# One of three GpSimd additions of a weight-product pair moved to VectorE, with the activation and the low half as steps of their own and attention units placed one by one

## The chip, the cores and the metric

One core of one Trainium2 chip runs the whole program in one launch. The metric is the device time in microseconds, the median of the runs. PE is TensorE, DVE is VectorE, ACT is ScalarE, POOL is GpSimd, and SP is the engine whose queue issues all the transfers.

## What is computed

Two stages in float32: an attention over q, k, v (8 batches, 8 heads, 576 positions, 64 wide), then a gated feed-forward layer.

```python
q_d, k_d, v_d = means over 4 neighbouring positions
out_d = softmax(q_d @ k_d.T / 8) @ v_d, repeated 4 times along the positions
out_local = softmax(masked(q @ k.T / 8, |i - j| < 4)) @ v
x = (out_up + out_local) as 4608 tokens x 512
y = (sigmoid(x @ w_gate) * (x @ w_val)) @ w_out        # 512 -> 1536 -> 512
```

## The kernel before, in words

**Units and batches.** The attention is done in 32 units of two heads (four units to a batch of 576 tokens). A unit's steps are named: `prep2`, `s0`, `s1`, `sm` (scores of the local part and their softmax), `d0`, `d1`, `dn` (the coarse part), `vd`, `v` (preparing v; `v` splits it into a high and a low float16 half, L191 on ACT and L192 on DVE, tile `vblk`), `a0`, `a1`, `at`, `od`, `x` (the two products, and the split of the result into float16 halves, L600 to L628). A float32 product of the feed-forward layer is three float16 matmuls (high by high, high by low, low by high).

**Batches 0 and 1** multiply the gate and value weights plainly (`moe_gate`, `moe_val`), while the weights are loaded, scaled and split (batch 0) and summed for what follows (batch 1, `sums`, L736 to L746).

**Batches 2 to 7** use a scheme with seven products in place of eight for a 2 by 2 block. `pair(b, n)` does one such block: n runs from 0 to 11, even n for the gate (PSUM tiles `pg`), odd n for the value (`pv`), two chunks of 128 hidden columns each. The seven products P1, P6, P7, P2, P5, P3, P4 are seven groups of six matmuls; in the rows a group is named by two digits: 00, 44, 55, 11, 33, 62, 26 in that order (`pg_4_5_44` is product P6 of batch 4's sixth gate pair). Each group's result is a 128 by 288 PSUM tile. ACT copies the first three to SBUF (L789, L792, L796, tiles of `arena` named `sx`), and DVE adds the other four from PSUM (L782, `plus`). Three additions have both operands in SBUF and run on POOL (also L782): P6's copy plus P1's, P7's copy plus that sum, and the fourth result from the second. At the end of an even pair ACT takes a tanh; at the end of an odd pair DVE multiplies (L679), ACT writes the high half of the product (L191) and DVE the low half (L192) into `gq`, which the output product reads.

**PSUM.** All groups of the layer take turns in five PSUM buffers (`ps_m`), the attention's other products in three (`ps_a`), so a group must wait until the group five before it has been read.

**Order.** After a batch's 12 pairs come its output products `po` (288 matmuls, tiles m = 0 to 3, halves h = 0, 1; L700 to L709). The four units of batch b+1 run meanwhile, between the groups of batch b. Every step stands at a position from the table `T` (`add(pos, f)`): a batch starts at `start(b)`, a pair's steps are a seventh of a pair apart, and a unit's step stands at the batch's start plus a number of its unit (`c0` to `c3`) plus a number of the step that all units share (`ms0`, `ms1`, ...). The steps are issued in that order, and a scheduler then fixes the order on each engine. Each engine works its own queue in order.

The lines that the argument uses: L413 (all products), L478, L489, L496 to L500 (local softmax), L521 to L541 (coarse softmax), L187 (largest value of v), L782 (`plus`), L192, L679.

## Time and profile before

| | us |
|---|---|
| median of 3 runs | 1086.05 |
| range of the runs | 1085.66 to 1088.92 |
| the profiled execution | 1082.34 |
| its span, first to last instruction | 1080.4 |
| PE busy in the span | 1025.9 (95%) |
| DVE busy | 744.7 (69%) |
| POOL busy | 610.7 (57%) |
| ACT busy | 488.1 (45%) |

[...] The profiled execution is 3.71 us shorter than the median. Matmuls are pipelined and their ends are modelled, so that PE can look busy through a short wait. In the views below, PEld is the loading of weights into PE. A busy share over the whole span mixes stages with different limits, so the windows by stage say more than the totals.

### The profile page before, as it was taken

The numbers are of one execution on the slowest core, as the hardware profiler recorded it, in microseconds if no ns is written. First come the engines' busy times: TensorE is split into PE (matmuls) and PEld (weight loads), VectorE is DVE, ScalarE is ACT, GpSimd is POOL, SyncE is SP. The second block draws the span as 40 slices with busy tenths as digits, with TensorE's granted clock in tenths as the row PEclk, the third lists the DMA queues.
The fourth block names the chain that finished last, engine by engine and source line by source line (L and its number), as shares of the span: only waits on it lengthen the run. The fifth ranks groups of instructions, "written<-read, shape, count | busy, mean of one in ns | idle before, by whom it ended". The sixth has DMA issues, their size and how long they took to land.

```text
span 1080.4 us, 23529 instructions
## 1 busy us (share of the span) xinstructions
PE 1025.9 (95%) x9511; PEld 810.3 (75%) x9511; DVE 744.7 (69%) x1366; ACT 488.1 (45%) x1089; POOL 610.7 (57%) x647
## 2 busy tenths in 40 slices
...
GB/s 371 138 234 269 279 140 122 110 120 125 122 109 186 171 206 190 81 134 223 182 166 121 142 211 182 120 129 170 211 175 112 131 217 152 107 34 114 171 46 34
DMA packets 64188, 168.99 MB, mean 156 GB/s; under 512 B 25040, under 2 KB 31312, under 8 KB 64080
## 3 DMA queue, kind: packets, MB, share of 16 engines
...
## 4 chain that ended last, share of the span: by engine, by line
PE 58%; DVE 19%; POOL 9%; issue 5%; ACT 5%; DMA 3%; SPq 0%; POOLq 0%; DVEq 0%; ACTq 0%
PE po L413 26%; PE pg L413 11%; PE pv L413 10%; POOL arena L782 4%; PE x L413 3%; PE s L413 2%; PE od L413 2%; POOL t L490 2%; DVE vm L187 1%; PE sd L413 1%; DVE arena L782 1%; DMA qkd<-in_qkd_dram 1%; DVE arena L742 1%; DVE tanh L679 1%; DVE gq L192 1%
## 5 line engine op out<-in xcount | busy, mean ns | idle before, releaser
L413 PEld LDWEIGHTS <-arena 128*128 128x128 f16 x4176 | 404.7, 98 | 129.5 <-issue 13.9
L413 PE MATMUL pg<-arena 128*128 128x288 f16 x2088 | 282.4, 290 | 12.2 <-DVE arena L782 5.2
L413 PE MATMUL po<-gq,wo 128*128 128x288 f16 x2304 | 292.1, 287 | 0.4 <-DVE arena L782 0.3
L413 PE MATMUL pv<-arena 128*128 128x288 f16 x2088 | 281.8, 287 | 2.0 <-DVE arena L782 0.6
L413 PEld LDWEIGHTS <-wo 128*128 128x128 f16 x2304 | 224.9, 98 | 58.1 <-issue 1.0
L782 POOL TENSOR_TENSOR arena<-arena 128x288 f32<-128x288 f32 x198 | 195.5, 995 | 67.8 <-ACT arena L792 52.4
L782 DVE TENSOR_TENSOR arena<-pv,arena 128x288 f32<-128x288 f32 x144 | 62.6, 444 | 59.1 <-POOL arena L782 49.2
L705 DVE TENSOR_SCALAR arena<-po,osc 128x288 f32<-128x288 f32 x32 | 16.5, 515 | 102.7 <-PE po L413 102.7
L192 DVE SCALAR_TENSOR_TENSOR vblk<-v,svb,vblk 64x640 f16<-64x640 f32 x48 | 76.0, 1583 | 4.2 <-ACT vblk L191 3.4
L490 POOL TENSOR_TENSOR t<-t,mx 128x640 f32<-128x640 f32 x32 | 49.6, 1551 | 51.5 <-DVE mx L489 51.0
L402 POOL TENSOR_TENSOR qkd<-qkd 128x576 f32<-128x576 f32 x29 | 39.0, 1345 | 51.3 <-DMA qkd<-in_qkd_dram 51.1
L191 ACT ACTIVATE gq<-tanh 128x576 f16<-128x576 f32 (+1 forms) x42 | 37.4, 890 | 62.6 <-DVE tanh L679 62.6
L288 POOL TENSOR_TENSOR arena<-arena 128x512 f16<-128x512 f32 x24 | 37.0, 1562 | 44.2 <-ACT arena L287 44.1
L413 PEld LDWEIGHTS s<-qk 64*64 64x64 f32 x1200 | 43.4, 137 | 17.6 <-issue 15.1
L192 DVE SCALAR_TENSOR_TENSOR gq<-tanh,gq 128x576 f16<-128x576 f32 (+1 forms) x42 | 52.8, 1256 | 4.0 <-ACT gq L191 4.0
L413 PE MATMUL s<-qk 64*64 64x64 f32 x1200 | 54.4, 227 | 0.0
L500 POOL TENSOR_TENSOR t<-t,sm 128x640 f32<-128x640 f32 x27 | 36.1, 1340 | 31.6 <-DVE sm L498 26.0
L413 PE MATMUL sd<-kdblk,qks 128*72 128x288 f32 x128 | 43.2, 420 | 10.3 <-DVE t L478 6.1
L707 ACT ACTIVATE arena<-po,osc 128x288 f32<-128x288 f32 x32 | 16.0, 500 | 81.6 <-PE po L413 62.4
L541 POOL TENSOR_TENSOR ad<-e,sme 72x288 f32<-72x288 f32 x50 | 33.4, 688 | 27.7 <-DVE sme L532 19.2
L524 ACT ACTIVATE e<-sd,mxd 72x144 f32<-72x144 f32 x128 | 46.9, 369 | 1.4
L191 ACT ACTIVATE vblk<-v,svb 64x640 f16<-64x640 f32 x48 | 39.6, 825 | 12.3 <-DVE svb L184 6.0
...
## 6 DMA issues: line engine op xcount, KB each, us to landing
...
```

Of the source, the lines that this page charges most:

```text
L191: nc.scalar.activation(hi, src, AF.Copy, scale=sc)
L192: return nc.vector.scalar_tensor_tensor(out=lo, in0=src, scalar=sc, in1=hi, op0=ALU.mult, op1=ALU.subtract)
L288: nc.gpsimd.tensor_tensor(out=lo, in0=a, in1=hi, op=ALU.subtract)
L402: nc.gpsimd.tensor_tensor(out=x[:, :, 0:2], in0=x[:, :, 0:2], in1=x[:, :, 2:4], op=ALU.add)
L413: nc.tensor.matmul(o, w[a], x[c], start=first and i == 0, stop=last and i == len(pairs) - 1)
L490: nc.gpsimd.tensor_tensor(out=t, in0=t, in1=mx.unsqueeze(2).to_broadcast([P, NBLK, WIN]), op=ALU.subtract)
L500: eng.tensor_tensor(out=t, in0=t, in1=sm.unsqueeze(2).to_broadcast([P, NBLK, WIN]), op=ALU.mult)
L524: nc.scalar.activation(s["e"][:, qb, h, :], pt[:QM, h * SD : (h + 1) * SD], AF.Exp, bias=mx[:, h : h + 1], scale=QKSCALE / 16, accum_out=s ...
L541: eng.tensor_tensor(out=AD[:, qb].rearrange("p c h k -> p h c k")[:, :, :, :KC], in0=s["e"][:, qb].rearrange("p h (c k) -> p h c k", c=NKC ...
L705: nc.vector.tensor_scalar(out=dst_, in0=pt[:, :HN], scalar1=sc, scalar2=None, op0=ALU.mult)
L707: nc.scalar.activation(dst_, pt[:, :HN], AF.Copy, scale=sc)
L782: eng.tensor_tensor(out=dst_, in0=x, in1=y, op=ALU.add)
```

## The change

In `pair`, the sum of P6 and P1 is one DVE addition that reads P6 from PSUM; the ACT copy and the POOL addition that did it are gone. P5's sum goes to `sx[:, 0]` and no longer into the result tile. The tanh, or the multiplication and the high half, become an eighth step (`act`) and the low half a ninth (`low`), placed 0.3 and 1.8 sevenths of a pair behind step `s4`'s place (rounded), so behind the first groups of the next pair. The output product starts with three pieces of ten chunks (m, h = 0,0; 0,1; 1,0) and then does the last two chunks of each; before, it started with two. In the table, the four units of a batch have their own 14 numbers each.

Other numbers that moved: the last output weight's place `j35` and the start of batch 1 `T1` are both 2.37 earlier, the places of two units with them; the first unit's steps are 0.83 later; eight matmuls on an idle tile stand at position 44 (`an3=8`). The engine of a few single operations of batches 0 and 1 changes: unit 1's coarse normalisation goes from ACT to DVE (`ae1`), unit 4's from DVE to ACT (`ae4`), units 2's and 6's from ACT to POOL; the local normalisation of units 3 and 6 goes from POOL to DVE (`te3`, `te6`).

```diff
         def s6():
-            nc.scalar.copy(sx[:, 1], go(P6))
-            plus(sx[:, 1], sx[:, 1], sx[:, 0], nc.gpsimd)
+            plus(sx[:, 1], go(P6), sx[:, 0])
...
         def s5():
-            plus(j["c"][:, 1], go(P5), sx[:, 1])
-            plus(j["c"][:, 3], j["c"][:, 1], sx[:, 2], nc.gpsimd)
+            plus(sx[:, 0], go(P5), sx[:, 1])
+            plus(j["c"][:, 3], sx[:, 0], sx[:, 2], nc.gpsimd)
 
         def s3():
-            plus(j["c"][:, 1], go(P3), j["c"][:, 1])
+            plus(j["c"][:, 1], go(P3), sx[:, 0])
 
         def s4():
             plus(j["c"][:, 2], go(P4), sx[:, 3])
+
+        def act():
             t = tg[b, p]
...
             act_val(t, j["c"])
-            del tg[b, p]
-            split(*[gq[:, 2 * p : 2 * p + 2, e].rearrange("p f (h c) -> p f h c", h=2) for e in range(2)],
-                  t.rearrange("p (f h) c -> p f h c", f=2), GSC)
-
-        return s1, s6, s7, s2, s5, s3, s4
+            nc.scalar.activation(gpart(p, 0), halves(t), AF.Copy, scale=GSC)
+
+        def low():
+            if k:
...
+                nc.vector.scalar_tensor_tensor(
+                    out=gpart(p, 1), in0=halves(tg.pop((b, p))), scalar=GSC, in1=gpart(p, 0), op0=ALU.mult, op1=ALU.subtract)
+
+        return s1, s6, s7, s2, s5, s3, s4, act, low
...
-        return start(b) + T[f"c{hp}"] * span(b - 1) / 126 + T["m" + k]
+        return start(b) + T[f"m{hp}{k}"] * span(b - 1) / 118
...
-                add(t0 + GP * i / 7, f)
+                add(t0 + GP * (i / 7 if i < 7 else (6.01 + (T["da"] if i == 7 else T["da"] + T["dl"])) / 7), f)
...
-        add(t0, lambda b=b, f=part: f(b, 0, 0, range(10)))
-        add(t0 + 0.4 * u0, lambda b=b, f=part: f(b, 0, 1, range(10)))
-        add(t0 + 0.8 * u0, lambda b=b, f=part: f(b, 0, 0, range(10, 12)))
-        add(t0 + 0.9 * u0, lambda b=b, f=part: f(b, 0, 1, range(10, 12)))
...
+        for i in range(3):
+            add(t0 + 0.4 * u0 * i, lambda b=b, i=i, f=part: f(b, i // 2, i % 2, range(10)))
+        for i in range(3):
+            add(t0 + (1.2 + 0.1 * i) * u0, lambda b=b, i=i, f=part: f(b, i // 2, i % 2, range(10, 12)))
```

**Place 1: DVE in the value pair 4 of batch 4** (`pv_4_4`; units 20 to 23 are the next batch's, and the pairs of batches 3, 5 and 6 read alike). Before:

```order
L600 TENSOR_TENSOR arena_109<-x_21_0_8556,od16_21_8512 128x464
L600 TENSOR_TENSOR arena_109<-x_21_8_8582,od16_21_8512 128x112
L192 SCALAR_TENSOR_TENSOR vblk_129<-v22_7472,svb_139,vblk_129 64x10x64
L782 TENSOR_TENSOR arena_109<-pv_4_4_33_8597,arena_109 128x288
L478 SCALAR_TENSOR_TENSOR t_23_8619<-s_23_0_8606,mk_108 128x384
L192 SCALAR_TENSOR_TENSOR vblk_129<-v22_7472,svb_139,vblk_129 64x10x64
L187 TENSOR_REDUCE vm6_9206<-v24_9068 128x1
L478 SCALAR_TENSOR_TENSOR t_23_8619<-s_23_3_8621,mk_108 128x256
L605 TENSOR_TENSOR arena_109<-arena_109 128x2x288
L187 TENSOR_REDUCE vm6_9206<-v25_9107 128x1
L489 TENSOR_REDUCE mx_23_8631<-t_23_8619 128x10
L782 TENSOR_TENSOR arena_109<-pv_4_4_26_8643,arena_109 128x288
```

After the change, the same pair from its first addition to the same last one:

```order
L783 TENSOR_TENSOR arena_109<-pv_4_4_44_8492,arena_109 128x288
L783 TENSOR_TENSOR arena_109<-pv_4_4_11_8509,arena_109 128x288
L783 TENSOR_TENSOR arena_109<-pv_4_4_33_8517,arena_109 128x288
L783 TENSOR_TENSOR arena_109<-pv_4_4_62_8530,arena_109 128x288
L478 SCALAR_TENSOR_TENSOR t_23_8551<-s_23_0_8538,mk_108 128x384
L478 SCALAR_TENSOR_TENSOR t_23_8551<-s_23_3_8553,mk_108 128x256
L489 TENSOR_REDUCE mx_23_8563<-t_23_8551 128x10
L783 TENSOR_TENSOR arena_109<-pv_4_4_26_8567,arena_109 128x288
```

What stood there of unit 21's result (`x_21`, L600, L605), of unit 22's split (`vblk`) and of the next v (L187) has gone to other places. Unit 21's result and unit 22's split now stand in the last pair, `pv_4_5`:

```order
L600 TENSOR_TENSOR arena_109<-x_21_0_8678,od16_21_8590 128x464
L600 TENSOR_TENSOR arena_109<-x_21_8_8704,od16_21_8590 128x112
L783 TENSOR_TENSOR arena_109<-pv_4_5_44_8719,arena_109 128x288
L192 SCALAR_TENSOR_TENSOR vblk_129<-v22_7449,svb_139,vblk_129 64x10x64
L783 TENSOR_TENSOR arena_109<-pv_4_5_11_8736,arena_109 128x288
L192 SCALAR_TENSOR_TENSOR vblk_129<-v22_7449,svb_139,vblk_129 64x10x64
L521 TENSOR_REDUCE mxd_23_1_8859<-sd_23_1_8857 72x2
L605 TENSOR_TENSOR arena_109<-arena_109 128x2x288
L550 TENSOR_TENSOR at16_22_8671<-at_22_3_8821,at16_22_8671 128x232
L783 TENSOR_TENSOR arena_109<-pv_4_5_33_8749,arena_109 128x288
L605 TENSOR_TENSOR arena_109<-arena_109 128x4x288
L783 TENSOR_TENSOR arena_109<-pv_4_5_26_8766,arena_109 128x288
```

Behind these, the output product of the batch begins on PE.

**Place 2: DVE in the value pair 2 of batch 4** (`pv_4_2`), where unit 20's result comes and unit 21's v is split. Before:

```order
L600 TENSOR_TENSOR xs_113<-x_20_0_8150,od16_20_8113 128x464
L600 TENSOR_TENSOR xs_113<-x_20_8_8176,od16_20_8113 128x112
L192 SCALAR_TENSOR_TENSOR vblk_129<-v21_7470,svb_139,vblk_129 64x10x64
L782 TENSOR_TENSOR arena_109<-pv_4_2_11_8196,arena_109 128x288
L192 SCALAR_TENSOR_TENSOR vblk_129<-v21_7470,svb_139,vblk_129 64x10x64
L605 TENSOR_TENSOR arena_109<-xs_113,arena_109 128x288
L782 TENSOR_TENSOR arena_109<-pv_4_2_33_8204,arena_109 128x288
```

After the change:

```order
L600 TENSOR_TENSOR xs_113<-x_20_0_8118,od16_20_8116 128x464
L783 TENSOR_TENSOR arena_109<-pv_4_2_44_8104,arena_109 128x288
L600 TENSOR_TENSOR xs_113<-x_20_8_8144,od16_20_8116 128x112
L192 SCALAR_TENSOR_TENSOR vblk_129<-v21_7447,svb_139,vblk_129 64x10x64
L521 TENSOR_REDUCE mxd_21_1_8224<-sd_21_1_8222 72x2
L192 SCALAR_TENSOR_TENSOR vblk_129<-v21_7447,svb_139,vblk_129 64x10x64
L605 TENSOR_TENSOR arena_109<-xs_113,arena_109 128x288
L783 TENSOR_TENSOR arena_109<-pv_4_2_11_8164,arena_109 128x288
L531 TENSOR_SCALAR sme_21_8067<-sme_21_8067 72x4
L783 TENSOR_TENSOR arena_109<-pv_4_2_33_8172,arena_109 128x288
```

The addition of group 44 (L783) is new, and a reduction of unit 21's coarse scores (L521) has come in between the two halves of the split.

**Place 3: DVE in batch 1**, ahead of the scores of unit 11 (`s_11_0`), around the value product of hidden chunk 6. Before:

```order
L605 TENSOR_TENSOR arena_109<-arena_109 128x2x288
L679 SCALAR_TENSOR_TENSOR tanh_112<-tanh_112,pv_1_6_1_3590 128x288
L605 TENSOR_TENSOR arena_109<-arena_109 128x4x288
L187 TENSOR_REDUCE vm3_4293<-v12_4155 128x1
L192 SCALAR_TENSOR_TENSOR gq_111<-tanh_112,gq_111 128x576
L742 TENSOR_TENSOR arena_109<-arena_109 128x256 x2
L187 TENSOR_REDUCE vm3_4293<-v13_4163 128x1
L187 TENSOR_REDUCE vm3_4293<-v14_4243 128x1
L478 SCALAR_TENSOR_TENSOR t_11_3648<-s_11_0_3635,mk_108 128x384
```

After the change:

```order
L679 SCALAR_TENSOR_TENSOR tanh_112<-tanh_112,pv_1_6_1_3544 128x288
L743 TENSOR_TENSOR arena_109<-arena_109 128x256
L187 TENSOR_REDUCE vm3_4257<-v12_4156 128x1
L192 SCALAR_TENSOR_TENSOR gq_111<-tanh_112,gq_111 128x576
L187 TENSOR_REDUCE vm3_4257<-v13_4158 128x1
L747 TENSOR_TENSOR arena_109<-arena_109 128x4x256
L478 SCALAR_TENSOR_TENSOR t_11_3606<-s_11_0_3593,mk_108 128x384
```

Unit 9's result (L605 twice) and one reduction of v (L187) no longer stand ahead of unit 11's scores.

## Rows read from the trace of the kernel before

**Rows 1.** The page's first part, the whole span: busy time and share of each engine, and its instructions.

```profile
PE 1025.9 (95%) x9511; PEld 810.3 (75%) x9511; DVE 744.7 (69%) x1366; ACT 488.1 (45%) x1089; POOL 610.7 (57%) x647
```

**Rows 2.** Windows by stage: start and end of the stretch, its length, then busy time and instructions of PE, PEld, DVE, ACT, POOL, then granted clock, DMA share, GB/s. The stages are batch 0, batch 1 with its output, the pairs and output of batches 2, 3, 4, 5, 6, the pairs of batch 7, and its output.

```profile
0.00:206.00 206.00, 182.40 (x1599) 144.68 (x1600) 172.28 (x377) 118.15 (x278) 113.03 (x116) 0.94 0.63 215
206.00:356.50 150.50, 143.14 (x1369) 114.08 (x1369) 115.89 (x194) 60.76 (x130) 74.25 (x67) 0.98 0.36 123
356.50:481.00 124.50, 121.04 (x1163) 95.53 (x1162) 85.15 (x153) 56.73 (x132) 84.42 (x89) 1.00 0.48 166
481.00:605.80 124.80, 120.98 (x1162) 95.09 (x1161) 83.84 (x149) 56.32 (x126) 78.26 (x88) 1.00 0.47 161
605.80:730.60 124.80, 120.95 (x1162) 95.09 (x1160) 85.67 (x149) 56.32 (x126) 78.07 (x88) 1.00 0.47 162
730.60:855.95 125.35, 121.15 (x1161) 95.14 (x1160) 83.78 (x149) 56.32 (x126) 77.90 (x88) 1.00 0.47 160
855.95:979.60 123.65, 119.11 (x1118) 93.51 (x1117) 77.44 (x136) 54.16 (x120) 70.10 (x76) 1.00 0.36 124
979.60:1041.40 61.80, 61.80 (x505) 49.25 (x504) 34.79 (x57) 26.22 (x47) 33.29 (x35) 1.00 0.40 139
1041.40:1080.40 39.00, 35.34 (x289) 27.98 (x286) 5.87 (x9) 3.16 (x5) 1.40 (x2) 1.00 0.09 31
```

**Rows 3.** Windows of batch 4, the same columns: first and last quarter of its pairs, and all its pairs.

```profile
605.80:626.50 20.70, 20.70 (x192) 15.82 (x190) 15.55 (x32) 9.55 (x21) 14.37 (x19) 1.00 0.58 192
667.80:690.00 22.20, 18.46 (x191) 14.29 (x189) 21.70 (x31) 12.38 (x32) 15.71 (x18) 1.00 0.42 151
605.80:690.00 84.20, 80.35 (x754) 61.93 (x752) 67.95 (x117) 45.41 (x106) 64.90 (x72) 1.00 0.54 186
```

**Rows 4.** Timeline of PE at the end of the pairs of batch 4: start, duration, instruction; in brackets the idle time before it and what ended it.

```profile
674.99 0.90 PE L413 MATMUL pg<-arena 128*128 128x288 f16 x6 [0.97 <-DVE arena L782]
...
677.90 0.71 PE L413 MATMUL sd<-kdblk,qks 128*72 128x288 f32 x2 [1.20 <-DVE t L478]
...
680.83 1.63 PE L413 MATMUL pg<-arena 128*128 128x288 f16 x12 [0.76 <-DVE arena L782]
```

**Rows 5.** Timeline of DVE in the same stretch; the split of v (`vblk`) is the second row.

```profile
668.68 0.81 DVE L600 TENSOR_TENSOR arena<-x,od 128x464 f32<-128x464 f32 x2
669.67 4.90 DVE L192 SCALAR_TENSOR_TENSOR vblk<-v,svb,vblk 64x640 f16<-64x640 f32 x1 [0.17 <-ACT vblk L191]
...
674.86 0.54 DVE L478 SCALAR_TENSOR_TENSOR t<-s,mk 128x384 f32<-128x384 f32 x1
675.43 1.23 DVE L192 SCALAR_TENSOR_TENSOR vblk<-v,svb,vblk 64x640 f16<-64x640 f32 x1
...
677.43 0.41 DVE L478 SCALAR_TENSOR_TENSOR t<-s,mk 128x256 f32<-128x256 f32 x1
...
679.61 0.80 DVE L489 TENSOR_REDUCE mx<-t 128x10 f32<-128x640 f32 x1
680.34 0.44 DVE L782 TENSOR_TENSOR arena<-pv,arena 128x288 f32<-128x288 f32 x1
```

**Rows 6.** Timeline of POOL in the same stretch.

```profile
669.73 0.79 POOL L782 TENSOR_TENSOR arena<-arena 128x288 f32<-128x288 f32 x1
...
673.83 1.39 POOL L628 TENSOR_TENSOR arena<-arena 128x288 f32<-128x288 f32 x1
```

**Rows 7.** Timeline of DVE earlier in the same batch: the second half of another unit's split, and the low half of a result.

```profile
644.08 0.89 DVE L192 SCALAR_TENSOR_TENSOR vblk<-v,svb,vblk 64x640 f16<-64x640 f32 x1
645.00 0.94 DVE L605 TENSOR_TENSOR arena<-xs,arena 128x288 f16<-128x288 f32 x1
```

**Rows 8.** Groups by line of DVE in the pairs of batch 4: count, busy time, mean ns of one, idle time before and what ended it.

```profile
L782 DVE TENSOR_TENSOR arena<-pv,arena 128x288 f32<-128x288 f32 x20 | 8.8, 442 | 4.3 <-POOL arena L782 4.3
```

**Rows 9.** Groups by line of POOL (first) and of ACT (second) in the same stretch.

```profile
L782 POOL TENSOR_TENSOR arena<-arena 128x288 f32<-128x288 f32 x32 | 31.2, 984 | 7.7 <-ACT arena L792 4.4 <-DVE arena L782 2.2 <-ACT arena L796 0.4
...
L792 ACT COPY arena<-pv 128x288 f32<-128x288 f32 x6 | 2.4, 402 | 0.3 <-PE pv L413 0.3
```

**Rows 10.** Waits in the pairs of batch 4: total, times, longest.

```profile
DVE arena L782 <- POOL arena L782: 4.6, 7, 1.4
```

**Rows 11.** The chain that ended last, in the pairs of batch 7: start, duration, instructions.

```profile
1000.17 5.14 PE pg L413 x42
```

**Rows 12.** Windows of batch 1, columns as in the second group.

```profile
297.00:310.00 13.00, 8.63 (x58) 6.22 (x57) 12.22 (x23) 5.26 (x13) 4.44 (x5) 0.87 0.11 42
258.00:271.00 13.00, 10.34 (x101) 7.60 (x99) 10.24 (x14) 3.93 (x7) 7.57 (x9) 0.87 0.47 149
```

**Rows 13.** Waits of PE in batch 1: total, times, longest.

```profile
PE at L556 <- DVE t L478: 4.4, 1, 4.4
```

**Rows 14.** Windows of batch 0, columns as in the second group.

```profile
52.00:156.00 104.00, 91.46 (x751) 69.68 (x749) 100.36 (x223) 55.40 (x112) 54.19 (x42) 0.95 0.73 230
156.00:169.00 13.00, 9.82 (x90) 8.64 (x89) 11.96 (x24) 8.87 (x23) 7.89 (x10) 0.73 0.31 107
```

**Rows 15.** Groups by line of DVE over the span: the local and the coarse normalisation that run on DVE now.

```profile
L500 DVE TENSOR_TENSOR t<-t,sm 128x640 f32<-128x640 f32 x5 | 4.9, 972 | 0.1
...
L541 DVE TENSOR_TENSOR ad<-e,sme 72x288 f32<-72x288 f32 x2 | 1.9, 974 | 0.0
```

More of the change, by code (lines that the diff above doesn't have):

```diff
@@ L692, in out_group @@
     def out_group(b, m, h, pt, fcs):
+        assert issued(b, "v", fcs)
         for fc in fcs:
@@ L785, in s1 @@
             ready()
+            assert all((b, i, "act") in seen for i in range(n - 1)) and all((b, "v", 2 * i) in seen for i in range(p - 1))
             if k == 0:
@@ L802, in s5 @@
         def s5():
-            plus(j["c"][:, 1], go(P5), sx[:, 1])
-            plus(j["c"][:, 3], j["c"][:, 1], sx[:, 2], nc.gpsimd)
+            plus(sx[:, 0], go(P5), sx[:, 1])
+            plus(j["c"][:, 3], sx[:, 0], sx[:, 2], nc.gpsimd)
         def s3():
-            plus(j["c"][:, 1], go(P3), j["c"][:, 1])
+            plus(j["c"][:, 1], go(P3), sx[:, 0])
         def s4():
             plus(j["c"][:, 2], go(P4), sx[:, 3])
+        def act():
             t = tg[b, p]
+            seen.add((b, n, "act"))
             if k == 0:
@@ L815, in s4, with halves, gpart @@
             act_val(t, j["c"])
-            del tg[b, p]
-            split(*[gq[:, 2 * p : 2 * p + 2, e].rearrange("p f (h c) -> p f h c", h=2) for e in range(2)],
-                  t.rearrange("p (f h) c -> p f h c", f=2), GSC)
-        return s1, s6, s7, s2, s5, s3, s4
+            nc.scalar.activation(gpart(p, 0), halves(t), AF.Copy, scale=GSC)
+        def low():
+            if k:
+                seen.update((b, "v", 2 * p + i) for i in range(2))
+                nc.vector.scalar_tensor_tensor(
+                    out=gpart(p, 1), in0=halves(tg.pop((b, p))), scalar=GSC, in1=gpart(p, 0), op0=ALU.mult, op1=ALU.subtract)
+        return s1, s6, s7, s2, s5, s3, s4, act, low
+    def halves(t):
+        return t.rearrange("p (f h) c -> p f h c", f=2)
+    def gpart(p, e):
+        return gq[:, 2 * p : 2 * p + 2, e].rearrange("p f (h c) -> p f h c", h=2)
     steps = {}
@@ L854, in attention_moe @@
             add(T[f"aw{i}"], lambda n=T[f"an{i}"]: awake(n))
-    for g in ("p0", "p1", "p2", "p3", "q", "m"):
+    for g in ("p0", "p1", "p2", "p3", "q", "m0", "m1", "m2", "m3"):
         for chain in ("s0 s1 sm a0 a1 x", "prep2 d0 d1 dn at od x", "vd od", "v x"):
@@ L867, in attention_moe @@
             continue
-        p0 = at(u, "s0") - T["qs0" if b == 1 else "ms0"]
+        p0 = at(u, "s0")
         add(max(at(u - 2, "s1") + 0.1, p0 - T["lk"]), lambda u=u: load_qk(u))
@@ L871, in attention_moe @@
         add(max(at(u - 1, "vd") + 0.1, p0 - T["ll"]), lambda u=u: load_vd(u))
-        pb = start(b) + T["c0"] * span(b - 1) / 126
+        pb = start(b) + T["m0s0"] * span(b - 1) / 118
         pl = max(at(u - 4, "v") + 0.1, T["v4"] + T["vs4"] * hp if b == 1 else pb + T["vv"] + T["vvs"] * hp)
```

7 lines of the change are left out of this document (3 added, 4 removed).

## Prediction

> **What bounds the kernel now.** The page's totals say PE: 95% busy against 69% for DVE and 57% for POOL [rows 1]. That is an average, so I went on to the windows by stage. The pairs of batch 7 and its output have no attention beside them, and there PE is busy for 61.80 of 61.80 us; nothing is to be gained there. In the five stretches before, PE is idle for 3.46, 3.82, 3.85, 4.20 and 4.54 us (length less PE busy): 19.87 us together. Batch 1 has 150.5 - 143.14 = 7.36 us of idle PE, batch 0 has 206 - 182.40 = 23.6 [rows 2].
>
> Where in a batch is this idle time? The windows of batch 4 answer: its first quarter of pairs has none, its last has 22.20 - 18.46 = 3.74 of the 3.85, and in that quarter DVE is busy for 21.70 of 22.20 us, 98% [rows 3]. PE's timeline there shows gaps of 0.97, 1.20 and 0.76 us, each ended by a DVE instruction [rows 4]. So PE is the bound in most of a batch, and DVE in a short stretch. DVE's timeline shows why: from 668.68 to 680.78 it works off unit 21's result, both halves of unit 22's split, unit 23's scores and three reductions between the additions that free PSUM [rows 5]. One half of the split takes 4.90 us, while POOL runs without a pause from 669.73 to 675.22 [rows 6]; another takes 0.89 [rows 7]. What I read from these: a DVE split can be held while POOL adds, and the five PSUM buffers do not cover 12 us of late additions.
>
> **The change, part by part.**
>
> *One POOL addition and one ACT copy less, one DVE addition more, 72 times.* A POOL addition takes 984 ns and P6's copy 402 ns [rows 9]; a DVE addition from PSUM takes 442 ns [rows 8]. In a batch of 12 pairs POOL loses 11.8 us, ACT 4.8, and DVE gains 5.3. None of it is PE time. ACT's 4.8 us give nothing by themselves: ACT is busy for 45.41 of 84.20 us of pairs [rows 3]. POOL's part shortens a chain: DVE waited 4.6 us in 7 waits for POOL's additions in a batch's pairs [rows 10], and the first of the two sums that P5 and P7 need is now DVE's own. DVE's 5.3 us fit if spread: its load goes from 67.95 to 73.3 of 84.20 us [rows 3].
>
> *The units placed one by one.* This is the part that I expect to pay. In the stretch of place 1 DVE has now only five additions, two score steps and a maximum: 5 x 0.44 + 0.54 + 0.41 + 0.80 = 3.95 us [rows 5], against a pair's 42 matmuls in 5.14 us [rows 11], so DVE keeps up and the three gaps go. What stood there stands in the last pair, whose twelve shown rows need about 0.50 + 0.81 + 4 x 0.44 + 2 x 0.89 + 0.44 + 1.20 + 1.34 + 0.40 = 8.2 us (rows 5 and 7 where they have the operation; L605's two at most 2.5, the small ones estimated as an addition each), or 12.2 with one split stretched by 4.90 - 0.89 = 4.0. Behind it PE has the rest of that pair, 36 matmuls, and then 60 matmuls of output before a group needs the buffer of group 33: 96 x 0.1224 = 11.8 us [rows 11]; the addition of 33 stands about 6 us into that list, 10 if stretched. This cover is why the heap costs nothing there. If the output's pieces were short of buffers, it would cost the excess, at most 1 us a batch.
>
> *A new narrow place.* In place 2 the addition of group 11 stands behind unit 20's result, the new addition of 44, a reduction, both halves of a split and a low half: 0.81 + 0.44 + 0.89 + 0.44 + 0.89 + 0.94 + 0.44 = 4.85 us [rows 5, 7]. PE asks for that buffer when it has done 55, 11, 33, 62, 26 and the next pair's 00: 36 matmuls, 4.4 us [rows 11], and some 0.6 us of attention products: 5.0. The slack is about 0.2 us. If no split is held, the new wait is 0; if one is held by 4.0, it is 3.8. Before, the second half of this place's split took 0.89 [rows 7], but POOL starts on the result at the same moment. I take the middle, 1.9 a batch, and keep both ends. Sum of batches 2 to 6: -19.9 + 5 x 1.9 = **-10.4** (ends -19.9 and -0.9).
>
> *Low half as a step of its own.* DVE now has an addition to do while ACT writes the high half; this is inside DVE's idle time and costed at nothing. Three pieces of output ahead of the last two chunks give the last low half 90 matmuls of cover, not 60 (11.0 against 7.3 us [rows 11]); the number of matmuls is the same.
>
> *Batch 1.* [...] I count the gap and its clock as gone: **-6.1**. The second gap, in 258 to 271, is 2.66 us and 1.7 of clock [rows 12]; it may go too (end: -10.5) or neither may (end: 0). The three additions a pair do not occur in this batch.
>
> *Batch 0.* Here DVE is busy for 100.36 of 104 us from 52 to 156 [rows 14], so what counts is DVE work. Unit 4's coarse normalisation leaves it: 2 x 0.974 = 1.9 us; unit 6's local one comes, 0.97 [rows 15]; units 1 and 3 lie before 52. Net **-1.0**. The eight idle matmuls stand ahead of a product that waits for weights; uncovered they cost at most 8 x 0.12 = 1.0. The other end is set by the clock: in 156 to 169 it was 0.73, 3.5 us lost [rows 14]. A moved gap can take that away or add it again: -4.5 to +3.5.
>
> *Queues.* POOL's unit steps are moved among its additions, and it waits for the next `qkd` from memory as before; the load is issued about 1.2 of the table's units earlier relative to the unit, and the one of `vd` about 8 earlier, both behind the previous unit's use of the same buffer. On SP the loads of the next v, two of which wait for DVE's splits, now stand between the weight loads singly. I cost these at 0; the cover is the three buffers of weights.
>
> **Sum:** -10.4 - 6.1 - 1.0 = -17.5 against the profiled execution's 1082.34: 1064.8. The runs' median is 3.71 above that execution; carried over, the forecast is 1086.05 - 17.5 = **1068.5 us**.
>
> **Rivals.**
>
> *The narrow place of each batch is hit in full* (0.20). For it: DVE has 5.3 us more, and the half of a split that met POOL took 4.90. Against it: POOL has 11.8 us less. Then batches 2 to 6 give 0.9 only, and the time is 1086.05 - 0.9 - 6.1 - 1.0 = **1078**.
>
> *DVE becomes the bound of the pairs, and the time grows* (0.12). DVE's pairs now are 67.95 busy and 16.25 idle [rows 3]. With 5.3 more, the stretch stays at 84.2 only if 5.3 of that idle time goes; that is the point from which it decides. If only the 4.6 us of waits for POOL go [rows 10], a batch grows by 0.7, five by 3.5: **1090**; if none goes, by 26, 1112. For it: the 98% of the last quarter. Against it: in the other three quarters DVE is at (67.95 - 21.70) / 62.0 = 75% [rows 3], and places 1 and 2 show the load spread. [...]
>
> *The gain is swallowed by batches 0 and 1* (0.10). Three new gaps like the one of batch 1, each 4.4 and 1.7 of clock, would cost 18.3: **1087**, no change. For it: their order is moved too, and DVE is at 96% in batch 0. Against it: no listed move adds DVE work there.
>
> That the change does less than it says is excluded by the order: the additions and places are there.
>
> **How the numbers follow.** My own case, 0.58, runs from no new wait and both gaps of batch 1 gone (-19.9 - 10.5 - 1.0, 1055) to most of the new wait (1074). With the first rival, 0.78 lie under 1082.8, which is faster by over 0.3% (3.3 us, about what a measurement of this kernel can tell from no change); I put some of the swallowed case there: 0.80. Same 0.09, slower 0.11. The range 1055 to 1084 takes in my case, the first rival and the near part of the third; it leaves out the second, and a little on either side.
>
> **What would show it.** Right: POOL's additions fall from three to two a pair; the last quarter of pairs has DVE under 95% and PE idle under 1 us; a batch takes 121 to 123 us, not 124.8; a `vblk` row of 3 us or more, if any, stands in the third or the last value pair; the 4.4 us wait of batch 1 is gone. Wrong: PE waits for L783 all over the pairs, DVE above 90% in every quarter, or new gaps with a clock under 1 in the first 356 us.

## The result and the profile after

The change is faster: 1053.97 us (median of 4 runs, 1047.1 to 1058.87) against 1085.86 (4 runs, 1081.47 to 1088.92), ratio 0.9705 with a 95% interval of 0.9641 to 0.9769. That is 31.9 us, where 17.5 were forecast, and the time lies 1 us below the range. The profiled execution took 1054.16 us (span 1052.4), 28.2 less than the one before.

The page's first line, which answers to [rows 1]:

```profile
PE 1017.3 (97%) x9519; PEld 810.7 (77%) x9519; DVE 745.5 (71%) x1440; ACT 457.1 (43%) x1009; POOL 560.5 (53%) x577
```

The windows by stage of the changed kernel, same columns and stages as [rows 2]:

```profile
0.00:206.00 206.00, 181.55 (x1599) 142.82 (x1600) 174.31 (x378) 115.35 (x270) 111.69 (x117) 0.95 0.64 215
206.00:357.50 151.50, 144.47 (x1378) 115.46 (x1377) 113.12 (x197) 60.61 (x130) 81.64 (x71) 0.98 0.36 129
357.50:477.10 119.60, 119.60 (x1163) 95.47 (x1161) 85.95 (x170) 52.05 (x115) 72.20 (x77) 1.00 0.49 168
477.10:596.30 119.20, 119.20 (x1160) 95.34 (x1159) 83.55 (x161) 51.42 (x115) 70.68 (x76) 1.00 0.49 169
596.30:715.50 119.20, 119.20 (x1160) 95.35 (x1159) 83.76 (x161) 51.54 (x115) 70.62 (x76) 1.00 0.48 170
715.50:834.70 119.20, 119.20 (x1160) 95.34 (x1159) 83.77 (x161) 51.56 (x115) 70.68 (x76) 1.00 0.49 169
834.70:951.50 116.80, 116.80 (x1115) 93.44 (x1114) 76.54 (x140) 50.06 (x113) 59.69 (x61) 1.00 0.37 128
951.50:1013.30 61.80, 61.80 (x506) 49.37 (x505) 39.29 (x70) 21.34 (x35) 23.18 (x24) 1.00 0.40 139
1013.30:1052.40 39.10, 35.46 (x290) 28.08 (x287) 5.25 (x7) 3.17 (x5) 0.14 (x1) 1.00 0.09 32
```

Read it stage by stage against [rows 2]. Batches 2 to 6 went from 623.1 to 594.0 us, and PE has no idle time left in them. (That is 29.1 us between the edges of these windows, and 28.6 when a batch is timed from its first gate group to the next batch's, as in the table further down.) The stretch before them is 1.0 us longer, batch 7 with its output 0.1. So the whole gain of the profiled execution lies in batches 2 to 6. Note the busy time too: PE was busy for 120.95 us in batch 4 with 1162 instructions, and is for 119.20 with 1160. The same work shows 1.75 us less busy time. The matmuls themselves are not faster: in both kernels the layer's matmuls of batch 4 start 0.123 us apart (mean of some 750 each). A wait hides part of itself in the modelled end of the matmul before it: at the 0.97 us gap of [rows 4] the next matmul starts 1.14 us later than that distance, and each of the batch's six gaps hides 0.16 us in this way. That is 1.0 of the 1.75 us; the other 0.8 was not taken apart.

Batch 4, last quarter of the pairs and all pairs, which answers to [rows 3]:

```profile
654.60:674.03 19.43, 19.43 (x208) 15.68 (x206) 17.23 (x33) 11.32 (x23) 16.79 (x19) 1.00 0.39 142
596.30:674.03 77.73, 77.73 (x746) 61.46 (x745) 62.25 (x118) 39.89 (x93) 53.98 (x58) 1.00 0.54 192
```

DVE is busy for 17.23 of 19.43 us in the last quarter (89%; 98% before) and for 80% of all pairs. Its timeline shows the splits of v at place 2 (pair 2) and in the last pair, where the split of place 1 stands now:

```profile
630.57 0.87 DVE L192 SCALAR_TENSOR_TENSOR vblk<-v,svb,vblk 64x640 f16<-64x640 f32 x1
631.36 0.44 DVE L521 TENSOR_REDUCE mxd<-sd 72x2 f32<-72x288 f32 x1
631.83 0.94 DVE L192 SCALAR_TENSOR_TENSOR vblk<-v,svb,vblk 64x640 f16<-64x640 f32 x1
...
671.40 1.30 DVE L192 SCALAR_TENSOR_TENSOR vblk<-v,svb,vblk 64x640 f16<-64x640 f32 x1 [1.23 <-ACT vblk L191]
672.63 0.44 DVE L783 TENSOR_TENSOR arena<-pv,arena 128x288 f32<-128x288 f32 x1
673.10 0.89 DVE L192 SCALAR_TENSOR_TENSOR vblk<-v,svb,vblk 64x640 f16<-64x640 f32 x1
```

No half takes over 1.30 us here, against 4.90 in [rows 5]. Groups by line of POOL (first) and DVE in the pairs of batch 4, which answer to [rows 9] and [rows 8]:

```profile
L783 POOL TENSOR_TENSOR arena<-arena 128x288 f32<-128x288 f32 x20 | 19.8, 993 | 11.5 <-DVE t L478 4.5 <-ACT arena L797 3.8 <-DVE arena L783 1.1
...
L783 DVE TENSOR_TENSOR arena<-pv,arena 128x288 f32<-128x288 f32 x27 | 12.0, 452 | 6.9 <-PE pv L413 5.0 <-ACT arena L791 1.7
```

DVE's additions now wait for PE (5.0 us) and once for ACT (1.7), no longer for POOL [rows 10]: in the pairs TensorE sets the time.

### The profile page after: what moved, and what is told of

Same layout as the page of the kernel before. It is cut to its first block, busy times and chain, and to the rows that moved or that the text cites. A ratio compares the mean times of both kernels' runs of the same rounds, so it can differ in the third digit from the quotient of the medians.

```text
span 1052.4 us, 23645 instructions
## 1 busy us (share of the span) xinstructions
PE 1017.3 (97%) x9519; PEld 810.7 (77%) x9519; DVE 745.5 (71%) x1440; ACT 457.1 (43%) x1009; POOL 560.5 (53%) x577
## 4 chain that ended last, share of the span: by engine, by line
PE 76%; DVE 14%; ACT 3%; POOL 2%; issue 2%; DMA 2%; SPq 0%; ACTq 0%; DVEq 0%; POOLq 0%
PE po L413 26%; PE pv L413 19%; PE pg L413 18%; PE s L413 4%; PE x L413 3%; PE sd L413 2%; PE od L413 2%; PE at L556 1%; DVE gq L192 1%; DVE hmx L187 1%; DVE wo L192 1%; DVE arena L743 1%; DVE tanh L679 1%; DVE wo L244 1%; PE adt L566 1%
## 5 line engine op out<-in xcount | busy, mean ns | idle before, releaser
L413 PE MATMUL pg<-arena 128*128 128x288 f16 x2088 | 277.8, 287 | 7.9 <-ACT arena L287 3.5
L783 POOL TENSOR_TENSOR arena<-arena 128x288 f32<-128x288 f32 x126 | 128.1, 1021 | 107.1 <-ACT arena L797 59.5
L783 DVE TENSOR_TENSOR arena<-pv,arena 128x288 f32<-128x288 f32 x180 | 80.5, 452 | 48.6 <-PE pv L413 38.8
L541 POOL TENSOR_TENSOR ad<-e,sme 72x288 f32<-72x288 f32 x54 | 54.1, 1019 | 22.0 <-DVE sme L532 12.7
L490 POOL TENSOR_TENSOR t<-t,mx 128x640 f32<-128x640 f32 x32 | 43.9, 1372 | 34.8 <-DVE mx L489 31.1
L192 DVE SCALAR_TENSOR_TENSOR vblk<-v,svb,vblk 64x640 f16<-64x640 f32 x48 | 54.0, 1124 | 6.9 <-ACT vblk L191 5.6
L783 DVE TENSOR_TENSOR arena<-pg,arena 128x288 f32<-128x288 f32 x126 | 54.4, 447 | 5.9 <-PE pg L413 3.9
L500 POOL TENSOR_TENSOR t<-t,sm 128x640 f32<-128x640 f32 x25 | 36.3, 1452 | 32.5 <-DVE sm L498 26.1
L402 POOL TENSOR_TENSOR vd<-vd 128x384 f32<-128x384 f32 x29 | 25.1, 866 | 48.1 <-DMA vd<-in_vd_dram 47.8
L791 ACT COPY arena<-pg 128x288 f32<-128x288 f32 x36 | 14.3, 397 | 75.2 <-PE pg L413 75.2
L404 POOL TENSOR_TENSOR vdblk<-vd 64x192 f32<-64x192 f32 x58 | 40.6, 700 | 4.0 <-PE od L413 1.0
```

The lines of the kernel that those rows point to most:

```text
L192: return nc.vector.scalar_tensor_tensor(out=lo, in0=src, scalar=sc, in1=hi, op0=ALU.mult, op1=ALU.subtract)
L402: nc.gpsimd.tensor_tensor(out=x[:, :, 0:2], in0=x[:, :, 0:2], in1=x[:, :, 2:4], op=ALU.add)
L404: eng.tensor_tensor(out=o, in0=x[ps, g, 0], in1=x[ps, g, 1], op=ALU.add)
L413: nc.tensor.matmul(o, w[a], x[c], start=first and i == 0, stop=last and i == len(pairs) - 1)
L490: nc.gpsimd.tensor_tensor(out=t, in0=t, in1=mx.unsqueeze(2).to_broadcast([P, NBLK, WIN]), op=ALU.subtract)
L500: eng.tensor_tensor(out=t, in0=t, in1=sm.unsqueeze(2).to_broadcast([P, NBLK, WIN]), op=ALU.mult)
```

## The experiments

A total says little here, because what lies ahead of batch 2 differs between profiled executions. So for each kernel this table has, from PE's timeline, the start of batch 2 (its first `pg` group) and the length of batches 2 to 6 (from there to batch 7's first), beside the ratio of the times.

| kernel | batch 2 starts | batches 2 to 6 | ratio (95%) |
|---|---|---|---|
| before | 356.8 | 622.6 | 1 |
| after, five parts | 357.6 | 594.0 | 0.9705 (0.9641 to 0.9769) |
| no_place | 366.0 | 618.7 | 0.9978 (0.9946 to 1.0009) |
| no_add | 354.3 | 618.2 | 0.9944 (0.9905 to 0.9984) |
| only_place | 359.1 | 620.2 | 0.9969 (0.9942 to 0.9997) |
| only_add | 355.3 | 617.7 | 0.9934 (0.9907 to 0.9960) |
| two | 358.4 | 594.0 | 0.9722 (0.9698 to 0.9745) |
| no_t0 | 355.4 | 594.0 | 0.9733 (0.9710 to 0.9756) |
| only_t0 | 361.7 | 623.2 | 0.9999 (0.9965 to 1.0032) |
| np_less_pool | 357.1 | 611.3 | one run |
| add_copy | 358.8 | 597.1 | one run |
| pool_load | 353.2 | 605.7 | one run |
| add_two | 354.4 | 603.7 | 0.9791 (0.9758 to 0.9825) |
| x9 | 354.6 | 598.9 | 0.9772 (0.9749 to 0.9795) |
| na_less_pool | 351.0 | 618.3 | one run |
| na_less_pool2 | 356.0 | 612.2 | one run |

How far such a length can be trusted is seen from kernels that differ only in parts that turn out to have no effect in these batches: after, two and no_t0 agree to 0.1 us; no_add and only_place differ by 2.1 us over the five batches, no_place and only_add by 1.0, before and only_t0 by 0.6. Single batches of such twins differ by up to 1.4 us in batch 2 and up to 1.0 in the others.

### Which part pays: four runs with one part undone or alone

The five parts are the moved addition, the places, the low half as a step, the third piece of output, and the other numbers of the table. no_place puts the shared numbers back in the changed kernel, and with them the distances of the loads (`lk`, `ll`, `vv`); no_add puts the ACT copy and the POOL addition back:

```diff
-        return start(b) + T[f"m{hp}{k}"] * span(b - 1) / 118
+        return start(b) + T[f"c{hp}"] * span(b - 1) / 126 + T["m" + k]
...
-            plus(sx[:, 1], go(P6), sx[:, 0])
+            nc.scalar.copy(sx[:, 1], go(P6))
+            plus(sx[:, 1], sx[:, 1], sx[:, 0], nc.gpsimd)
...
```

only_place and only_add make the same two edits the other way in the kernel before.

> The changed kernel with the units' steps back at the shared table (one set of 14 numbers and four starts); all other parts stay. A batch of the changed kernel takes 119.2 us (477.1 to 596.3), one of the kernel before 124.8. Theory A (the places pay): the heap of DVE work in the value pair 4 is back, PE waits there again, and a batch takes 123 us or more; five batches are 19 us longer or more, the time is 1073 or above. Theory B (the shorter chain of additions pays): a batch takes 119 to 121 us, the time is 1054 to 1063. Rival C (neither alone: the extra DVE addition on top of the old heap makes it worse than before): a batch takes more than 124.8 us, the time is above 1082.

> The changed kernel with P6's sum back as an ACT copy and a POOL addition (three POOL additions a pair); the units stay placed one by one. Theory A (the places pay): a batch takes 119 to 121 us, the time is 1054 to 1063. Theory B (the shorter chain pays): DVE waits for POOL's additions again (4.6 us a batch before), POOL's busy time in the pairs rises by 11.8 us, and a batch takes 123 us or more, the time is 1073 or above.

> The kernel before with the units placed one by one (their 14 numbers each), nothing else. Theory A (the places pay): a batch falls from 124.8 to 121 us or less, the time from 1086 to 1067 or less. Theory B (the chain pays): a batch stays at 123 to 125 us, the time at 1077 to 1087.

> The kernel before with P6's sum as one DVE addition from PSUM (two POOL additions a pair), nothing else. Theory A (the places pay): the heap in the value pair 4 stays and has one addition more; a batch stays at 123 to 126 us, the time at 1077 to 1092. Theory B (the chain pays): fewer POOL additions also hold the split in the heap for less; a batch falls to 121 us or less, the time to 1067 or less.

Neither theory holds: no_place and only_add came out nearer to theory A, no_add and only_place to theory B. Undoing either part loses nearly everything (24.7 and 24.2 of 28.6 us); doing either alone gains little (2.4 and 5.0). Batch by batch it is sharper. In batches 2 to 5 the places alone gain 0.3 us and the addition alone loses 1.0, while both gain 21.8. Batch 6 differs: there the addition alone gains 5.9 of the 6.8 us (123.6 to 117.7) and the places alone 2.1. Beside batch 6 no reduction of a next v (L187) stands in DVE's queue, where batch 4 has four; whether that is the reason was not tested.

The traces show two different narrow places. In no_place, windows of a twelfth of batch 4's pairs (the last three) and what DVE and POOL do from 680.6 us on (a row without brackets has no idle time of 0.15 us or more before it):

```profile
681.15:688.17 7.02, 5.30 (x49) 3.93 (x45) 6.96 (x5) 2.64 (x5) 6.34 (x8) 1.00 0.31 107
688.17:695.18 7.01, 5.31 (x41) 3.54 (x39) 7.01 (x11) 2.20 (x8) 3.07 (x3) 1.00 0.65 230
695.18:702.20 7.02, 5.58 (x43) 4.05 (x42) 7.02 (x14) 3.20 (x10) 4.54 (x3) 1.00 0.17 71
```

```profile
680.61 6.14 DVE L192 SCALAR_TENSOR_TENSOR vblk<-v,svb,vblk 64x640 f16<-64x640 f32 x2
...
680.59 0.79 POOL L783 TENSOR_TENSOR arena<-arena 128x288 f32<-128x288 f32 x1
681.34 0.79 POOL L625 TENSOR_TENSOR arena<-arena 128x288 f32<-128x288 f32 x1
682.09 1.37 POOL L626 TENSOR_TENSOR arena<-arena,xs 128x288 f32<-128x288 f32 x1
683.43 1.14 POOL L402 TENSOR_TENSOR qkd<-qkd 128x576 f32<-128x576 f32 x1
684.53 0.78 POOL L783 TENSOR_TENSOR arena<-arena 128x288 f32<-128x288 f32 x1
685.28 0.78 POOL L628 TENSOR_TENSOR arena<-arena 128x288 f32<-128x288 f32 x1
```

That is the heap of [rows 5], with PE idle for 4.9 us and DVE full. In no_add PE's longest wait in batch 4 stands elsewhere, in the third quarter. Window, then DVE, POOL and PE there, and DVE's waits for POOL's additions in all pairs of batch 4 (total, times, longest):

```profile
658.74:665.62 6.88, 5.52 (x54) 4.30 (x52) 6.44 (x6) 2.04 (x4) 6.88 (x7) 1.00 0.97 358
```

```profile
662.34 3.39 DVE L826 SCALAR_TENSOR_TENSOR gq<-arena,gq 128x1152 f16<-128x1152 f32 x1
...
661.73 1.28 POOL L541 TENSOR_TENSOR ad<-e,sme 72x288 f32<-72x288 f32 x2
662.98 0.78 POOL L783 TENSOR_TENSOR arena<-arena 128x288 f32<-128x288 f32 x1
663.73 0.78 POOL L783 TENSOR_TENSOR tanh<-tanh,arena 128x288 f32<-128x288 f32 x1
664.48 2.26 POOL L402 TENSOR_TENSOR qkd<-qkd 128x576 f32<-128x576 f32 x1
...
666.15 1.02 PE L413 MATMUL pv<-arena 128*128 128x288 f16 x7 [1.89 <-DVE tanh L783]
```

```profile
DVE arena L783 <- POOL arena L783: 7.1, 9, 1.5
```

Here POOL is full (6.88 of 6.88 us). The new places put unit 22's two normalisations (L500, L541) among three additions a pair, and DVE's low half (L826 here, L825 in the changed kernel), in a stretch of POOL work without a pause, took 3.39 us and holds up the addition that PE needs. DVE's waits for POOL's additions have grown too, from 4.6 us in the pairs [rows 10] to 7.1. So the new places alone exchange one narrow place for another.

### Are these two parts enough: two

The kernel before with the two parts alone.

> The kernel before with exactly two of the five parts: P6's sum on DVE and the units placed one by one; the low half, the output's first pieces and the other numbers of the table as before. Alone, each of the two gave a batch of 123.5 to 124.0 us (124.5 before, 118.8 with all five parts; mean of batches 2 to 6 each time). Theory D (two narrow places, each enough by itself: DVE's heap in the last quarter and POOL's chain in the third): a batch takes 118.8 to 119.8 us. Rival E (the low half as a step or the output's third piece is needed too): a batch takes 121 us or more.

594.0 us, as with all five. Theory D holds; the low half as a step, the third output piece and the other numbers bring nothing that these runs can tell from nothing.

### Why DVE is late: np_less_pool

```diff
-            nc.gpsimd.tensor_tensor(out=tf[:, 1], in0=own[:, 1], in1=tf[:, 0], op=ALU.subtract)
+            if b < 5 or hp != 1:
+                nc.gpsimd.tensor_tensor(out=tf[:, 1], in0=own[:, 1], in1=tf[:, 0], op=ALU.subtract)
```

(and so for `tf[:, 2]` and `tf[:, 3]`, L626 and L628)

> The changed kernel with the shared table of places (run no_place), without three POOL subtractions of the second unit's result (L625, L626, L628) from batch 5's units on, so beside batches 4, 5 and 6; that part of the result is left out. In no_place the two halves of the split in batch 4's value pair 4 took 2.19 and 3.91 us while POOL ran without a pause for 7 us. Theory H (POOL holds the split): with the pause the halves take under 1.5 us each, and the batches 4, 5 and 6 are 2 us shorter or more than the 124.8 of batch 4 in no_place, while batches 2 and 3 stay. Rival I (the heap is too long by its own clean work): the halves may be shorter, but a batch stays within 1 us.

Both halves of the split in batch 4 and POOL's pause beside the second, and the windows of that batch here and in no_place:

```profile
671.03 2.24 DVE L192 SCALAR_TENSOR_TENSOR vblk<-v,svb,vblk 64x640 f16<-64x640 f32 x2
...
672.60 1.67 POOL L402 TENSOR_TENSOR qkd<-qkd 128x576 f32<-128x576 f32 x1 [0.93 <-DMA qkd<-in_qkd_dram]
```

```profile
606.91:728.07 121.16, 119.51 (x1161) 95.32 (x1159) 87.25 (x160) 51.09 (x114) 65.93 (x73) 1.00 0.48 167
```

```profile
617.99:742.78 124.79, 119.94 (x1162) 95.01 (x1159) 88.47 (x160) 51.10 (x114) 69.49 (x76) 1.00 0.48 162
```

2.24 us for the two, not 6.14, and DVE has as many instructions (160). Batch 4 is 3.6 us shorter, batch 5 2.0 (124.2 to 122.2), batch 3, where nothing was left out, 0.7 longer. Batch 6 did not move (117.8 to 118.2); its halves had taken 1.17 and 1.31 us in no_place already. So POOL held the split. Against the changed kernel's 119.2 us that was most of what the heap cost in batch 4 (3.6 of 5.6) and less than half in batch 5 (2.0 of 5.0). Two cautions. Without the three instructions a few DVE instructions also stand in another order. And a held split is not late by itself: before the change one half took 3.71 us in the first quarter of batch 4's pairs, where PE has no idle time [rows 3].

### What the third addition on POOL cost: add_copy, pool_load, na_less_pool, na_less_pool2

add_copy keeps ACT's copy of P6 and makes the sum on DVE from SBUF. pool_load adds POOL work to the changed kernel:

```diff
+            for i in range(2):
+                plus(junk, sx[:, 2, i * HN // 2 : (i + 1) * HN // 2], junk, nc.gpsimd)
```

> The changed kernel with P6's copy still on ACT and its sum on DVE from SBUF: the POOL addition is gone, the ACT copy is not. Theory H (POOL's back-to-back work holds DVE's long SBUF instructions, in no_add the low half with 3.39 us): a batch takes 118.8 to 120.5 us as in the changed kernel. Rival J (the copy's latency, or ACT's 4.8 us, is what the third addition cost): a batch takes 122 us or more as in no_add (123.6).

> The changed kernel with two added POOL additions of 128 x 144 in each pair, on a tile that nothing else uses, queued behind the sum of P7: POOL's load is back near that of the kernel before (about 0.9 us a pair, 10.8 us a batch, estimated from two of its 144-wide rows of 0.45 us), the chain of sums that DVE waits for has no link more. Theory K (POOL's load as such: it runs without a pause and holds DVE's long instructions): a batch takes 122 us or more, with a DVE row of 3 us or more in the third quarter of the pairs. Rival L (the chain: DVE's additions wait for POOL's sums one after another): a batch stays at 119.2 to 120.5 us.

add_copy: 119.4 us a batch on average (118.8 in the changed kernel, 123.6 in no_add), so the copy costs about 0.6 and the POOL addition the rest, 4.2; the low half at the place of no_add's long one takes 1.36 us. pool_load: POOL is as busy as in no_add (63.1 and 61.9 us in the pairs of batch 4), and the batch takes 121.6, 2.4 more than the changed kernel, between the two bounds; no DVE row in the second half of the pairs is over 2 us. POOL's load as such can explain half of no_add's loss; the held instruction of theory K did not show.

The other half was asked of no_add itself, by leaving out two POOL normalisations:

```diff
-            eng.tensor_tensor(out=t, in0=t, in1=sm.unsqueeze(2).to_broadcast([P, NBLK, WIN]), op=ALU.mult)
+            if b < 5 or hp != 2:
+                eng.tensor_tensor(out=t, in0=t, in1=sm.unsqueeze(2).to_broadcast([P, NBLK, WIN]), op=ALU.mult)
...
+                if b >= 5 and hp == 2:
+                    continue
                 eng.tensor_tensor(
...
```

> The run no_add (three POOL additions a pair, units placed one by one) without POOL's two normalisations (L500, L541) of the second unit from batch 5's units on, so beside batches 4, 5 and 6; these factors are left out of the result. In no_add POOL worked without a pause from 654.6 to 667.5 us beside batch 4, a DVE low half took 3.39 us there, and TensorE waited 1.9 us for the addition behind it; batches 2 to 6 took 124.8, 124.6, 123.7, 123.8 and 121.3 us. Theory R (the crowding at this one place): the low half takes under 2 us, and batches 4, 5 and 6 fall by 1.5 us or more each, batches 2 and 3 stay. Rival L (the longer chain in all pairs): batches 4 to 6 fall by under 1 us.

> As na_less_pool, but the normalisations (L500, L541) of the third unit are left out, which in no_add are POOL's from 658.6 to 663.0 us; those of the second unit, left out in na_less_pool, lay elsewhere, and the low half took 3.50 us as before. Theory R (the crowding at this one place): the low half takes under 2 us, and batches 4, 5 and 6 (123.7, 123.8, 121.3 us in no_add) fall by 1.5 us or more each, batches 2 and 3 stay. Rival L (the longer chain in all pairs): batches 4 to 6 fall by under 1 us.

na_less_pool took the second unit's (`hp != 1`), which stand elsewhere, and so missed: the crowding stayed, and batches 4 to 6 took 124.7, 123.6 and 122.1 us. It serves as a control: less POOL work at another place brings nothing. na_less_pool2 took the right ones: 121.4, 122.6 and 119.1 us, 2.2, 1.2 and 2.2 less than no_add (the control above moved by up to 1.0). The low half in batch 4, first in na_less_pool, then in na_less_pool2, and PE's one wait that is left in the pairs there:

```profile
658.07 3.50 DVE L829 SCALAR_TENSOR_TENSOR gq<-arena,gq 128x1152 f16<-128x1152 f32 x1
```

```profile
663.08 1.59 DVE L829 SCALAR_TENSOR_TENSOR gq<-arena,gq 128x1152 f16<-128x1152 f32 x1 [0.50 <-ACT gq L824]
...
683.95 0.90 PE L413 MATMUL pv<-arena 128*128 128x288 f16 x6 [0.89 <-ACT arena L797]
```

Theory R holds for batches 4 and 6 and falls short of its bound in batch 5. About half of no_add's loss (4.5 us in batch 4) is the crowding at this place; 0.9 us is a wait for ACT's copy of P6, which the change removes; the rest, some 1.4 us, I did not take apart.

### How far it goes: add_two

```diff
-            plus(sx[:, 3], sx[:, 2], sx[:, 1], nc.gpsimd)
+            plus(sx[:, 3], sx[:, 2], sx[:, 1])
```

> The changed kernel with one POOL addition more moved to DVE (P7's sum; one POOL addition a pair is left). Theory M (TensorE sets batches 2 to 6 now): a batch stays at 119.2 us, the time at the changed kernel's (ratio 0.966 to 0.975). Rival N (DVE, with 5.3 us a batch more, becomes the bound in the value pair 5): a batch takes 120.5 us or more, the ratio is above 0.976.

Rival N holds in its numbers: 121.4 us in batch 4, ratio 0.9791. DVE is nearly full again in the last quarter. The last twelfth but one of batch 4's pairs, and the longest of PE's waits there:

```profile
665.40:672.10 6.70, 5.90 (x47) 4.40 (x46) 6.56 (x12) 3.88 (x10) 3.58 (x4) 1.00 0.34 106
...
669.25 0.90 PE L413 MATMUL pg<-arena 128*128 128x288 f16 x6 [0.67 <-DVE arena L783]
```

One addition moved is right for this order, two are too many. What was not separated is the time of this second sum from its kind: it reads both its operands from SBUF, unlike the first.

### Batches 0 and 1: no_t0, only_t0, x9

no_t0 and only_t0 take away, or make alone, the table's other numbers and engine choices. Among these are some that the list of the change leaves out: the last steps of units 4 to 7 (`v`, `at`, `od`, `x`) are 1.48 later and unit 2's `v` is 6.6 later.

> The changed kernel with the other numbers of the table (batches 0 and 1: first unit, T1, engines of single operations, the eight idle matmuls) back. Batches 2 to 6 keep their 594 us. Theory F (these numbers bring nothing): the start of batch 2 lies within 354 to 366 us, as in all runs so far, and the time is within 5 us of the changed kernel's ratio to the kernel before (0.9705), so 0.966 to 0.975. Rival G (they brought about the 7 us that the prediction gave them): the ratio is 0.977 or above.

> The kernel before with only the other numbers of the table changed (batches 0 and 1). The prediction gave them 7.1 us: the ratio would be 0.9935 and batch 2 would start at about 350 us. Theory F (they bring nothing): batch 2 starts at 354 to 362 us, the ratio is 0.997 to 1.004. In either case a batch from the second on takes 124.5 us.

Theory F holds both times: 0.9733 against 0.9705 with intervals that overlap, and 0.9999. PE's second wait in batch 1 before the change (the first is in [rows 13]), then the waits in only_t0, then in the changed kernel:

```profile
PE pg L413 <- DVE tanh L679: 2.7, 1, 2.7
```

```profile
PE at L556 <- DVE t L478: 4.4, 1, 4.4
PE pg L413 <- DVE tanh L679: 2.9, 1, 2.9
PE po L413 <- ACT gq L191: 1.0, 1, 1.0
```

```profile
PE sd L413 <- ACT e L524: 3.3, 1, 3.3
PE po L413 <- ACT gq L191: 2.7, 1, 2.7
PE pg L413 <- DVE tanh L679: 0.8, 1, 0.8
```

The 4.4 us wait of [rows 13] went with the units' places (only_place lacks it, only_t0 has it), and came back as two: 3.3 in the pairs and 2.7 in the output, 6.8 together with the third, against 7.1 for the two of the kernel before and 8.3 for the three of only_t0. The clock came back with them: behind the 3.3 us wait the granted clock was 0.51 from 271.7 to 274.9 us, behind the 2.7 us wait 0.51 from 319.5 to 322.7, and 1.00 just before and after both stretches. It is 0.98 in the pairs of batch 1 and 0.96 in its output, where it was 0.96 and 1.00. For the 2.7 us wait, DVE and ACT of the changed kernel at the end of batch 1's pairs:

```profile
310.78 2.60 DVE L605 TENSOR_TENSOR arena<-arena 128x1152 f16<-128x1152 f32 x1 [0.24 <-ACT arena L604]
...
315.62 0.44 DVE L679 SCALAR_TENSOR_TENSOR tanh<-tanh,pv 128x288 f32<-128x288 f32 x1
...
316.80 0.68 ACT L191 ACTIVATE gq<-tanh 128x576 f16<-128x576 f32 x1 [4.02 <-DVE tanh L679]
```

Unit 9's low half, taken from ahead of unit 11's scores, now stands ahead of the last products that the output waits for. x9 moves it (and unit 10's split) behind them:

```diff
+        late = {(2, 1, "x"): 9, (2, 2, "v"): 4}.get((b, hp, k), 0)
+        return start(b) + T[f"m{hp}{k}"] * span(b - 1) / 118 + late
```

> The changed kernel with unit 9's result 9 later and unit 10's split of v 4 later in the table, for these two units of batch 1 alone. Theory P (the 4.4 us wait of batch 1 has come back as a wait of the output for the last gq halves, 2.7 us, because unit 9's long low half L605 and unit 10's split now stand ahead of the last products on DVE): the wait of po for ACT's L191 falls under 0.5 us, the output stage of batch 1 from 46.2 to 43.5 us, and the time by 2.7 us, to a ratio of about 0.968. Rival Q (PE finds another wait behind it): the output stage stays within 1 us of 46.2, or the pairs of batch 2 give it back.

Rival Q holds. The output stage of batch 1 fell from 46.2 to 43.9 us and the 2.7 us wait is gone, but batch 2's first products then wait for unit 9's result, and its pairs take 82.9 us, not 78.0:

```profile
PE pg L413 <- ACT arena L604: 1.9, 1, 1.9
PE pg L413 <- DVE arena L605: 1.1, 1, 1.1
```

## Why the prediction was wrong, point by point

The time lies 1 us below the range, which is less than the runs scatter (1047.1 to 1058.87). Inside it would have been luck: batches 2 to 6 gained 29.1 us where 10.4 were forecast, and batches 0 and 1 nothing where 7.1 were.

**The step that failed first** is "None of it is PE time", the price of the moved addition. The prediction looked for PE's idle time before the change, found it in one quarter [rows 3], and took the place of that heap as the whole of it. It did not ask what POOL's queue looks like under the new places. It had the wait that grows there in its rows (DVE for POOL's additions, 4.6 us) and put it at nothing. With three additions a pair, POOL is full in one twelfth of the pairs (6.88 of 6.88 us), those waits are 7.1 us, and no_add loses 24.2 of the 28.6 us. The addition's worth is not a share of the gain: each part gains 2 to 5 us alone, both together 28.6, and in batches 2 to 5 neither gains anything alone. Of the rivals, the first had the right form (a new narrow place in each batch), but on DVE in place 2; the real one was POOL's, and the change takes it away itself.

**The second** is the size of what can be saved, 19.9 us as length less PE busy. It was 29.1 (623.1 to 594.0). PE's busy time in these stages fell by 9.2 us as well, from 603.2 (sum of the five stages in [rows 2]) to 594.0, for the same number of instructions within 3 a stage. The ends of matmuls are modelled, and part of each wait shows as busy: 0.16 us at each gap, with the matmuls' distance unchanged at 0.123 us. That an end is modelled was known ahead, and the sum did not use it.

**The third** is the new narrow place 2, +9.5 us for five batches. It cost nothing: its splits took 0.87 and 0.94 us, the end of the range at which no split is held. The cause given was right (POOL holds a split: 6.14 us for its two halves in no_place, 2.24 in np_less_pool), the choice of the middle was not.

**The fourth** is -7.1 us for batches 0 and 1, which became +1.0. Of the -7.1, 6.1 are the 4.4 us gap of batch 1 [rows 13] and (1 - 0.87) x 13 = 1.7 us of clock [rows 12]: before the change the granted clock was 1.00 up to 301.9 us, 0.50 from 302.0 to 305.3 and 1.00 from 305.5 on. That the 1.7 us would go with the gap was the author's estimate; the changed kernel has two such stretches in batch 1, as the kernel before had (its other one was 0.51 from 264.4 to 267.7). The gap did go, as place 3 said, but what stood there was moved ahead of another consumer. "Name what is late next" was done for the heap of place 1 and not here. Batch 0's -1.0 can't be told at all: the start of batch 2 lies anywhere from 351.0 to 366.0 us in the 16 profiled executions.

The errors add up: -17.5 forecast, -9.2 (size), -9.5 (place 2), +8.1 (batches 0 and 1), +0.1 (batch 7) give -28.0, the difference of the spans. The runs' medians differ by 31.9; both lie within what the interval of the ratio allows, 25.1 to 39.0.

**Right:** the heap of place 1 and its cure; the cover of 96 matmuls behind the last pair (no wait there); low half and third output piece at nothing; POOL's hold on a split. DVE as the bound (second rival) did not come, but it was near: with one addition more DVE is nearly full again (add_two). In the heap it was POOL's work that made DVE late: the two halves of a split took 2.24 us without three of POOL's instructions, 6.14 with them.

The prediction's list of signs: additions fell to two a pair, the last quarter has DVE at 89% and PE idle at 0, no `vblk` row of batches 2 to 6 reaches 3 us (the longest is 2.46), the 4.4 us wait is gone. These four came true; the fifth, a batch of 121 to 123 us, did not (119.2). Signs that confirm a mechanism do not confirm its price.
